# A planner that counts a port shared by VectorE and GpSimd, with other durations and priorities; the splitting of token blocks on VectorE; a reordered end of a token block

## The chip, the core and the metric

The kernel runs on one core of one Trainium2 chip. The metric is the device time of one execution in microseconds (us), from the first to the last thing that the core does; smaller is better. The engines of the core are TensorE (PE in the rows; PEld is its weight load), VectorE (DVE), ScalarE (ACT), GpSimd (POOL) and SyncE (SP). SP computes nothing here: it issues almost all DMAs. Each engine works through its own list of instructions in order; between engines there are only semaphores.

## What is computed

Windowed attention (8 batches, 8 heads, 576 positions, 64 channels a head; four heads with a plain causal window of 32, four with a dilated one), then a mixing by two Fourier transforms, a normalisation, and a feed-forward layer (512 to 2048 to 512) with the residual added:

```python
scores = scale * np.matmul(q, k.transpose(0, 1, 3, 2))
scores = np.where(masks[None, :, :, :], scores, -1000000000.0)
scores = scores - np.max(scores, axis=-1, keepdims=True)
attn = np.exp(scores)
attn = attn / (np.sum(attn, axis=-1, keepdims=True) + 1e-09)
x = matmul(attn, v)                       # then (batch, seq, 512)
...
X = np.fft.fft(np.fft.fft(x, axis=1), axis=2)
u = x + np.real(X).astype(np.float32)
mu = np.mean(u, axis=-1, keepdims=True)
var = np.mean((u - mu) ** 2, axis=-1, keepdims=True)
un = (u - mu) / np.sqrt(var + 1e-06)
ch = np.maximum(un @ w_ch1, 0.0) @ w_ch2
return (u + ch).astype(np.float32)
```

## The kernel before

**Stages.** `attention` (L481) does each batch in twelve units (`attend`, L504): two score products into a bank `sc`, a masked minimum on VectorE (L521), exponentials on ScalarE (L527), four transposes (L540), a copy, four products with `v` (L547) and a division on VectorE, stored to DRAM. `mix` (L648) reads a batch back, folds it on GpSimd and VectorE, multiplies it by sequence and channel tables (`seq_sb`, `tail_sb`, `chn_sb`, `alt_sb`), and adds the result on GpSimd; `normalise` (L605) writes the rows `u`, with mean and scale in two more columns, to DRAM. The products are kept accurate by splitting each float32 operand in a rounded high part (a copy on ScalarE) and the remainder (a subtraction on VectorE or GpSimd); three products make one.

**The feed-forward layer** is in two parts. Five of the 16 hidden blocks (`wa1`, `wa2`) are done in the `fill` pieces (L1087), two token tiles each, as soon as their tiles are normalised; the sums go to DRAM as `parts`. The other eleven are done at the end for nine token blocks of 512 rows, in a loop over pairs of hidden blocks (`two_tiles`, L1227; `one_tile`, L1259) that uses sums and differences of halves of the tokens and of the weights to save products. The weights arrive as 64-bit words, and `words_of` (L834) makes float32 of them with four VectorE instructions (L857 to L866).

**A token block.** `load_blocks` (L1056) reads the 512 rows of a block in four DMAs (L1014), transposes them with four VectorE instructions (L1024), makes four sums or differences (`combine`, L1068, GpSimd), and splits seven pieces into `xb`: ScalarE makes each high part (L1078), and the remainder (L1081) is made by GpSimd for three pieces and by VectorE for four. `xb` exists once, so a piece is overwritten when its last product of the block before is done. For the first token block this has a late priority (`LAST`), for the others an early one (`SOON`).

**The end of a token tile** (`finish`, L963): the rows `u` come by DMA (L977, or an indirect one from GpSimd, L980), ScalarE adds the mean back (L983), the partial sums come by DMA (L985). When PE has closed the accumulation `acc`, VectorE adds acc and the partial sums (L986), and then multiplies by the row's scale and adds u (L988). The output DMAs follow: for the last block 16 of 64 KB, half on SP's queue, half on ScalarE's.

**The order of all work** is made on the host by a planner (`Plan`, L178): each `add` gives an engine, an estimated cost, what is read and written, a priority (smaller goes first) and, for a DMA, its bytes. `run` (L235) plays the program through in time: an engine that is free takes the ready operation of smallest priority number. A DMA is taken to land after 0.65 us, its bytes at 300 GB/s behind the DMAs before it, and 2.8 us. The lists of instructions of each engine are written in the order in which the planner started them; on the chip nothing else of the planned times is kept. The priority of attention is 12 b + u for unit u of batch b. That of other work is set against it by constants (L37 to L41): `P_QK0`, `P_QK`, `P_V` for loads of q, k, v; `P_W + P_WF f` for preparing the five fill weights f, whose DMAs have `P_WD` added; `P_MIX*` and `P_SPAN*` for the place and the length of a mix; `P_FILL` for the first fill. `T_SEQ` and `T_CHN` are the planned times from which the tables may be loaded (L470 to L477); these loads are in GpSimd's queue, which has nothing before them, and no semaphore holds them.

Of the kernel before, what the change touches and what calls it, by code (L numbers as in the profile page):

```python
# [19 lines left out]
P = 128  # L20
# [153 lines left out]
class Op:  # L174
    __slots__ = ("eng", "cost", "fn", "prio", "bufs", "after", "waits", "ready", "start", "num", "nbytes")


class Plan:  # L178
# [20 lines left out]
    def add(self, eng, cost, fn, r=(), w=(), prio=0.0, nbytes=0, at=0.0):  # L199
        op = Op()  # L200
        op.eng, op.cost, op.fn, op.prio, op.nbytes = eng, cost, fn, prio, nbytes
# [33 lines left out]
    def run(self):  # L235
# [15 lines left out]
        lanes = {e: [] for e in busy}  # L251

# [20 lines left out]
        while events:  # L273
# [67 lines left out]
def pe(n, m=P):  # L341
    return max(n / 2400 + 0.0025, m / 1200)
# [25 lines left out]
def fused_kernel(ctx: ExitStack, tc, q, k, v, w1, w2, seq, tail, chn, alt, mask, ident, perm, flip, out):  # L368
# [67 lines left out]
    def dma(fn, r, w, prio, nbytes, slow=1):  # L436
        return add("SP", 0.5, fn, r, w, prio, nbytes * slow)
# [3 lines left out]
    def start():  # L441
        dma(lambda: nc.sync.dma_start(out=mask_sb(), in_=mask), (), (mask_sb,), -7.9, QB * 3 * KB * 4)
        dma(lambda: nc.sync.dma_start(out=ident_sb(), in_=ident), (), (ident_sb,), -7.8, P * 3 * P * 4)
        dma(lambda: nc.sync.dma_start(out=perm_sb(), in_=perm), (), (perm_sb,), -7, QB * QB * 12)
# [33 lines left out]


# [24 lines left out]
    def attend(b, dil, j, u, tq, kb, vt, xt, prio):  # L504
# [3 lines left out]
        for n, t in enumerate(blocks):  # L508
# [7 lines left out]
            add("PE", 2 * pe(512), scores, (tq, kb), ((sc, n),), prio)  # L516
# [29 lines left out]
        for i in range(4):  # L546
            add("PE", 0.16, lambda i=i: nc.tensor.matmul(  # L547
# [57 lines left out]
    def normalise(u, idx, prio):  # L605
# [15 lines left out]
            out=uc()[:, C + 1:C + 2], in0=r0(), in1=r1(), op=ALU.mult), (r0, r1), ((uc, 2),), prio + 1)  # L621
# [693 lines left out]
```

## Time and profile before

| what | us |
|---|---|
| three runs: median (lowest to highest) | 1122.07 (1121.26 to 1122.24) |
| the profiled execution, whole | 1123.04 |
| the profiled execution, span of its instructions | 1121.3 |
| PE busy in that span | 1072.7 |
| VectorE, ScalarE, GpSimd busy | 726.6, 522.5, 289.4 |
| mean granted PE clock | 0.981 of full |

The profiled execution took 1.74 us more than its span and 0.97 us more than the median run. A row of the chip's trace names a line of the kernel, an engine, the operation, what it writes and reads, how many instructions were merged, and in brackets how long the engine was idle before it and what released it. The granted clock has two levels, 2.4 GHz (1.00 in the rows) and 1.2 GHz (0.50); a mean between them says how long each was granted in the stretch.

### The profile page before, as it was taken

Reading aid. Unit: us, or ns where it says so; the run is one execution under the profiler, and the core shown is the slowest. Engines: PE = TensorE matmul, PEld = TensorE weight load, DVE = VectorE, ACT = ScalarE, POOL = GpSimd, SP = SyncE. Lnnn points to the kernel's source line nnn. Section 1 sums busy time; section 2 is a strip of 40 time slices with the busy share of each in tenths; the row PEclk is TensorE's granted clock in tenths of the full one; section 3 lists DMA queues with packets and bytes.
Section 4 is the critical chain, followed back from the end, with each engine's and each line's share of the span. In section 5 each row is a group of like instructions: output and inputs, shape, how many; then the busy total and the mean of one; then the engine's idle time right before and its main releaser. Section 6 shows DMA issues by size and latency. Waiting matters only on the chain.

```text
span 1121.3 us, 20217 instructions
## 1 busy us (share of the span) xinstructions
PE 1072.7 (96%) x7066; PEld 948.1 (85%) x7066; DVE 726.6 (65%) x2318; ACT 522.5 (47%) x1331; POOL 289.4 (26%) x341
## 2 busy tenths in 40 slices
PE   5799999999999999999989899999999999999997
PEld 3567888889888988899978798898988889888886
DVE  5789988767867778867769763536363545454523
ACT  4587656546555634344435443333333333333331
POOL 2025365343434254300030421121202120212200
PEclk8799999999999999999999899999999999999999
DMA  9677567656655344345423250505050504041211
GB/s 313 175 207 220 159 193 195 193 143 184 176 165 149 115 136 123 110 122 152 129 87 114 66 160 1 150 1 151 1 150 1 142 9 132 20 107 45 93 59 38
DMA packets 104310, 137.05 MB, mean 122 GB/s; under 512 B 9656, under 2 KB 62328, under 8 KB 104208
## 3 DMA queue, kind: packets, MB, share of 16 engines
q1 hardware_dynamic: 100624, 126.85, 39.0%
q0 software_dynamic: 3040, 8.09, 2.4%
q8 instruction: 56, 0.92, 0.3%
q10 hardware_dynamic: 544, 0.82, 0.2%
q14 instruction: 46, 0.38, 0.1%
HBM read 97.92 MB, written 37.80 MB: 121 GB/s over the span
## 4 chain that ended last, share of the span: by engine, by line
PE 81%; DVE 11%; DMA 3%; issue 2%; POOL 1%; ACT 1%; SPq 0%; DVEq 0%; ACTq 0%; POOLq 0%
PE sc L942 15%; PE ff L1199 13%; PE mix L1199 8%; PE ff L926 7%; PE pt L942 6%; PE av L942 6%; PE ff L942 6%; PE sc L513 5%; PE av L547 5%; PE mix L775 2%; PE pt L540 2%; PE mix L729 2%; PE pt L926 2%; DVE pm L521 2%; DMA ut<-in_w_dram 1%
## 5 line engine op out<-in xcount | busy, mean ns | idle before, releaser
L527 ACT ACTIVATE pm<-pm,mx 96x128 f32<-96x128 f32 x384 | 130.3, 394 | 53.6 <-DVE mx L521 49.9
L1215 ACT COPY s<-ff 128x256 f32<-128x256 f32 x135 | 50.2, 373 | 163.9 <-PE ff L1199 163.5
L513 PE MATMUL sc<-kb,tq 128*96 128x256 f32 x384 | 109.4, 405 | 16.2 <-DMA kb<-in_k_dram 8.0
L926 PE MATMUL ff<-ut,wa 128*128 128x256 f32 x780 | 110.0, 291 | 3.3 <-DVE h L934 3.3
L521 DVE CUSTOM_DVE_ANT_0 pm<-sc,mask_sb 96x128 f32<-96x128 f32 x384 | 92.8, 278 | 24.4 <-PE sc L513 23.4
L942 PE MATMUL sc<-wa,h 128*128 128x512 f32 x420 | 106.4, 395 | 0.0
L926 PEld LDWEIGHTS ff<-ut,wa 128*128 128x128 f32 x780 | 99.7, 192 | 5.1 <-DVE h L934 3.9
L942 PE MATMUL ff<-wa,h 128*128 128x512 f32 x390 | 95.8, 397 | 0.0
L547 PEld LDWEIGHTS av<-vt,ptsb 128*96 128x96 f32 x768 | 79.9, 171 | 16.7 <-issue 5.5
L1068 POOL TENSOR_TENSOR ut<-ut 128x512 f32<-128x512 f32 x36 | 50.7, 1428 | 166.5 <-DVE ut L1024 86.4
L547 PE MATMUL av<-vt,ptsb 128*96 128x65 f32 x768 | 84.5, 253 | 6.9 <-DVE xt L559 5.3
L942 PEld LDWEIGHTS sc<-wa,h 128*128 128x128 f32 x420 | 76.2, 188 | 15.6
L942 PEld LDWEIGHTS ff<-wa,h 128*128 128x128 f32 x390 | 71.6, 188 | 15.7
L942 PE MATMUL sc<-wd,h 128*128 128x512 f32 x324 | 84.1, 394 | 0.0
L513 PEld LDWEIGHTS sc<-kb,tq 128*96 128x96 f32 x384 | 57.9, 173 | 30.0 <-issue 13.3
L1246 DVE TENSOR_TENSOR c<-s,s 128x256 f32<-128x256 f32 x45 | 22.3, 496 | 89.6 <-ACT s L1215 86.5
L1199 PEld LDWEIGHTS ff<-xb,pair 128*128 128x128 f32 x540 | 74.0, 189 | 6.6 <-ACT s L1215 0.7
L1024 DVE STREAM_TRANSPOSE ut<-ut 128x512 f32<-128x512 f32 (+1 forms) x76 | 71.7, 984 | 11.0 <-DMA ut<-us 10.9
L1199 PE MATMUL ff<-xb,pair 128*128 128x256 f32 x540 | 76.8, 281 | 0.5 <-ACT s L1215 0.5
L1081 POOL TENSOR_TENSOR xb<-ut,xb 128x512 fp32r<-128x512 f32 x27 | 36.8, 1363 | 133.5 <-ACT xb L1078 133.5
L1220 ACT ACTIVATE h<-row 128x256 fp32r<-128x256 f32 x90 | 37.5, 417 | 64.1 <-DVE row L1236 38.2
L980 POOL DMA_INDIRECT ut<-us,flip_sb x20 | 19.8, 988 | 180.9 <-DMA ut<-us 87.2
(158 smaller groups left out, 2318.4 us busy)
## 6 DMA issues: line engine op xcount, KB each, us to landing
vt<-in_v_dram SPq DMA_DIRECT2D x32, 390.0 KB
ut<-in_w_dram SPq DMA_DIRECT2D x20, 512.0 KB
us<-uc SPq DMA_DIRECT2D x36, 257.0 KB
tq<-in_q_dram SPq DMA_DIRECT2D x32, 288.0 KB
part<-row SPq DMA_DIRECT2D x36, 256.0 KB
ut<-us SPq DMA_DIRECT2D x36, 256.0 KB
ut<-part SPq DMA_DIRECT2D x36, 256.0 KB
kb<-in_k_dram SPq DMA_DIRECT2D x62, 144.0 KB
```

The source lines that it names most:

```text
L513: nc.tensor.matmul(sc()[:QB, 256 * n:256 * n + 256], lhsT=tq()[:, cols], rhs=kb()[:, :, keys], start=True, stop=True,)
L521: nc.vector.tensor_tensor_reduce(pm()[:, i], sc()[:QB, KB * i:KB * i + KB], mask_sb()[:, masks[blocks[i // 2]]], -0.125, 3.0e38, ALU.add, ...
L527: add("ACT", 0.295, lambda i=i: nc.scalar.activation(out=pm()[:, i], in_=pm()[:, i], func=AF.Exp, bias=mx()[:, i:i + 1], scale=-1.0), ((mx ...
L547: add("PE", 0.16, lambda i=i: nc.tensor.matmul(av()[:QB, 65 * i:65 * i + 65], lhsT=pt()[:, i], rhs=vt()[:, i % 2, blocks[i // 2]], start=T ...
L926: nc.tensor.matmul(z()[:, :n_tok], lhsT=wf()[:, a, kk], rhs=ut()[:, p, kk], start=(kk == 0 and n == 0), stop=(kk == KT - 1 and n == 2),)
L942: nc.tensor.matmul(acc(), lhsT=h()[:, a, P * s:P * s + P], rhs=wf()[:, p], start=(first and n == 0), stop=(last and n == 2),)
L1024: nc.vector.transpose(out=o[back], in_=x[:, g])
L1068: add("POOL", pool(C), lambda: nc.gpsimd.tensor_tensor(out=made(i)(), in0=x(), in1=y(), op=ALU.subtract), (*done, *((raw, ("s", j)) for j ...
L1081: add(eng, (pool if eng == "POOL" else dve)(C), lambda j=j, get=get, lo=lo: lo.tensor_tensor(out=xb()[:, j, 1], in0=get(), in1=xb()[:, j, ...
L1199: nc.tensor.matmul(z()[:, lo:lo + TOK1], lhsT=ap()[:, a, kk], rhs=xb()[:, j, p, kk], start=(start and k == 0), stop=(stop and k == 6 * len ...
L1215: add("ACT", act(TOK1), lambda: nc.scalar.copy(out=s(), in_=src()[:, :TOK1]), (src,), (s,), SOON - 1)
L1220: add("ACT", act(TOK1), lambda: nc.scalar.activation(out=h()[:, 0], in_=z(), func=AF.Relu), need, ((h, 0),), SOON)
```

## The change

No product and no token is added or left out. The change has five parts.

1. **Port.** An operation can carry the mark `port`: all computing of GpSimd has it, and many VectorE operations whose operands are all in SBUF. In the planner an operation with the mark starts only when no other marked one is running. No semaphore is added for it on the chip.
2. **Durations.** Several costs are other numbers; a DMA is taken to land after 0.45 us, its bytes at 340 GB/s and 0.6 us; a transpose of a token tile costs 1.0 in place of 0.6, and its loads count 1.25 times.
3. **Constants.** Nearly all priorities are other numbers. The mask and the identity now stand before, or level with, the first q. The mix of batch 0 is spread over 18.58 units in place of 8, later ones over 18.65 in place of 13. Fill weights start at 10.04, 9.28 apart, in place of 8.0 and 8.0.
4. **Tables.** Ahead of each table load VectorE writes one element of the table (`touch`), planned from `T_SEQ` (10.36) or `T_CHN` (24.62) on; GpSimd's DMA waits for it by semaphore.
5. **Token blocks.** All four `combine` and all seven remainders of `load_blocks` are VectorE's. In `finish` VectorE first makes partial sums times scale plus u, which needs no `acc`, and then acc times scale plus that.

The diff, cut to its core ("..." marks what is left out; marks and costs of the same kind as those shown are left out elsewhere):

```diff
-P_QK0, P_V0 = -8.0, -7.0
-P_ST, P_FD, P_WD, P_ST0, P_FD0, P_SPAN0, P_SPAN1 = -4.0, -12.0, -10.0, 0.0, 0.0, 8.0, 13.0
-P_QK, P_V, P_TR, P_MIX, P_SPAN, P_W, P_WF, P_FILL, P_FILLT = -8.0, -7.0, -5.0, 2.0, 13.0, 8.0, 8.0, 45.0, 4.0
-P_MIX0, P_MIX1 = 3.0, 0.0
-T_SEQ, T_CHN = 16.0, 24.0
+P_QK0, P_V0 = -7.8, -7.0
+P_ST, P_FD, P_WD, P_ST0, P_FD0, P_SPAN0, P_SPAN1 = -4.0, -21.87, -10.68, 0.0, 0.0, 18.58, 12.39
+P_QK, P_V, P_TR, P_MIX, P_SPAN, P_W, P_WF, P_FILL, P_FILLT = -8.0, -5.77, -5.0, 2.0, 18.65, 10.04, 9.28, 43.42, 4.0
+P_MIX0, P_MIX1 = 3.0, 0.93
+T_SEQ, T_CHN, T_STEP, P_SEQ, P_CHN = 10.36, 24.62, 1.0, -4.0, -2.0
+P_MASK, P_ID, P_PERM = -7.9, -7.8, -7.0
...
+        op.port = port or (eng == "POOL" and not nbytes)
...
-                        if place(ops[e[1]], now):
+                        if (not ops[e[1]].port or port <= now) and place(ops[e[1]], now):
...
+                    if got.port:
+                        port = end
...
-                        dma = max(dma, end + 0.65) + got.nbytes / 3.0e5
-                        done = dma + 2.8
+                        dma = max(dma, end + 0.45) + got.nbytes / 3.4e5
+                        done = dma + 0.6
...
+        def table(t, m, dst, src, prio, nbytes, at):
+            def touch():
+                nc.vector.memset(dst().bitcast(F32)[0:1, 0:1] if m is None else dst().bitcast(F32)[0:1, 0, 0:1], 0.0)
+            key = t if m is None else (t, m)
+            add("DVE", 0.065, touch, (), (key,), prio, at=at)
+            add("POOL", 0.53, lambda: nc.gpsimd.dma_start(out=dst(), in_=src), (), (key,), prio, nbytes)
+
         for i in range(2):
             for m in range(2):
-                add("POOL", 0.06, lambda i=i, m=m: nc.gpsimd.dma_start(out=seq_sb[i]()[:, m], in_=seq[i, m]),
-                    (), ((seq_sb[i], m),), 6 + i, P * 2 * NSP * 4, at=T_SEQ + i)
+                table(seq_sb[i], m, lambda i=i, m=m: seq_sb[i]()[:, m], seq[i, m], P_SEQ + i, P * 2 * NSP * 4, T_SEQ + i * T_STEP)
...
-        add("DVE", dve(C), lambda: nc.vector.tensor_tensor(
-            out=row(), in0=acc(), in1=row(), op=ALU.add), (acc,), (pk,), prio)
         add("DVE", 0.66, lambda: nc.vector.scalar_tensor_tensor(
-            row(), row(), u(C + 1, C + 2), u(0, C), op0=ALU.mult, op1=ALU.add), (uk,), (pk,), prio)
+            u(0, C), row(), u(C + 1, C + 2), u(0, C), op0=ALU.mult, op1=ALU.add), (pk,), (uk,), prio, port=True)
+        add("DVE", 0.66, lambda: nc.vector.scalar_tensor_tensor(
+            row(), acc(), u(C + 1, C + 2), u(0, C), op0=ALU.mult, op1=ALU.add), (uk, acc), (pk,), prio)
...
-                tuple((us[c], i0 + i) for i in range(n)), ((rb, ("raw", a)),), prio, 32 * 4 * n * 512)
+                tuple((us[c], i0 + i) for i in range(n)), ((rb, ("raw", a)),), prio, 32 * 4 * n * 512, slow=1.25)
...
-                add("DVE", 0.6 / len(steps), lambda i=i, g=g, back=back: turn(i, g, back), raws, done[-1:], prio)
+                add("DVE", 1.0 / len(steps), lambda i=i, g=g, back=back: turn(i, g, back), raws, done[-1:], prio)
...
-            add("POOL", pool(C), lambda: nc.gpsimd.tensor_tensor(out=made(i)(), in0=x(), in1=y(), op=ALU.subtract),
-                (*done, *((raw, ("s", j)) for j in after)), ((raw, ("s", i)),), prio)
+            add("DVE", dve(C), lambda: nc.vector.tensor_tensor(out=made(i)(), in0=x(), in1=y(), op=ALU.subtract),
+                (*done, *((raw, ("s", j)) for j in after)), ((raw, ("s", i)),), prio, port=True)
...
-            lo = nc.gpsimd if eng == "POOL" else nc.vector
-            add(eng, (pool if eng == "POOL" else dve)(C), lambda j=j, get=get, lo=lo: lo.tensor_tensor(
+            add("DVE", dve(C), lambda j=j, get=get: nc.vector.tensor_tensor(
                 out=xb()[:, j, 1], in0=get(), in1=xb()[:, j, 0].bitcast(F32), op=ALU.subtract),
-                (*need, (xb, (j, 0))), ((xb, (j, 1)),), prio)
+                (*need, (xb, (j, 0))), ((xb, (j, 1)),), prio, port=True)
...
-    def put_h(z, need):
+    def put_h(z, need, port=True):
```

## Rows read from the trace of the kernel before

**Rows 1.** The page's first part: busy time of an engine, its share of the span, and its instructions.

```profile
PE 1072.7 (96%) x7066; PEld 948.1 (85%) x7066; DVE 726.6 (65%) x2318; ACT 522.5 (47%) x1331; POOL 289.4 (26%) x341
```

**Rows 2.** Busy time by stretch, the whole span in eleven stretches: the stretch and its length in us; busy us and instructions of PE, PEld, DVE, ACT, POOL; then the mean granted PE clock, the busy share of the DMA engines, and GB/s.

```profile
0.00:8.04 8.04, 0.00 (x1) 0.03 (x1) 4.91 (x23) 1.28 (x1) 4.67 (x12) 1.00 0.85 225
8.04:36.00 27.96, 20.11 (x101) 14.74 (x102) 17.06 (x81) 14.10 (x37) 1.08 (x2) 0.80 1.07 309
36.00:84.00 48.00, 42.21 (x264) 31.75 (x263) 35.62 (x215) 34.97 (x103) 6.11 (x9) 0.87 0.63 188
84.00:240.00 156.00, 149.51 (x1147) 131.16 (x1146) 133.39 (x622) 99.46 (x277) 78.31 (x106) 1.00 0.64 187
240.00:430.00 190.00, 189.42 (x1375) 169.09 (x1374) 139.77 (x619) 102.47 (x282) 74.94 (x110) 1.00 0.54 156
430.00:560.00 130.00, 125.89 (x794) 112.63 (x794) 102.66 (x209) 54.11 (x122) 17.34 (x22) 0.99 0.40 120
560.00:590.00 30.00, 24.40 (x154) 22.21 (x154) 20.64 (x30) 13.08 (x32) 11.52 (x7) 0.94 0.26 88
590.00:630.00 40.00, 40.00 (x251) 35.86 (x250) 37.99 (x84) 20.80 (x53) 0.00 (x0) 1.00 0.42 119
630.00:645.00 15.00, 12.01 (x52) 10.08 (x51) 9.85 (x13) 6.04 (x12) 11.63 (x8) 0.77 0.08 19
645.00:1110.00 465.00, 465.00 (x2925) 417.58 (x2924) 219.48 (x420) 176.17 (x420) 83.76 (x69) 1.00 0.26 74
1110.00:1121.30 11.30, 4.10 (x18) 2.98 (x16) 5.22 (x8) 0.00 (x0) 0.00 (x0) 0.81 0.33 93
```

**Rows 3.** Instructions in order of time, from the start to 24 us: start, length, engine, line, operation, what it writes and reads, count, idle time before it and what ended that.

```profile
1.25 1.29 POOL L472 DMA_DIRECT2D seq<-in_seq_dram  x2 [0.82 <-POOLq L1303]
...
5.15 1.34 SPq L498 DMA_DIRECT2D tq<-in_q_dram  x1
...
8.04 2.84 PE L513 MATMUL sc<-kb,tq 128*96 128x256 f32 x6 [8.04 <-DMA kb<-in_k_dram]
...
9.64 3.23 SPq L854 DMA_DIRECT2D ut<-in_w_dram  x2
...
16.23 0.64 PE L513 MATMUL sc<-kb,tq 128*96 128x256 f32 x2 [1.89 <-DMA tq<-in_q_dram]
...
22.98 0.43 DVE L857 TENSOR_SCALAR ut<-ut 128x512 uint32<-128x512 uint32 x1 [3.87 <-DMA ut<-in_w_dram]
...
23.88 0.67 PE L513 MATMUL sc<-kb,tq 128*96 128x256 f32 x2 [2.91 <-DVE mx L521]
```

**Rows 4.** The issues of DMAs by line: what is written and read, the issuing queue, count, KB of each, and the median us from issue to landing.

```profile
seq<-in_seq_dram POOLq DMA_DIRECT2D x4, 290.0 KB, 9.5
```

**Rows 5.** Instructions in order of time, 559 to 571 us, of VectorE, GpSimd and PE; columns as in rows 3.

```profile
559.81 4.11 DVE L1081 TENSOR_TENSOR xb<-ut,xb 128x512 fp32r<-128x512 f32 x3
559.95 5.12 POOL L1068 TENSOR_TENSOR ut<-ut 128x512 f32<-128x512 f32 x3 [79.54 <-ACT xb L1078]
...
563.85 1.52 DVE L857 TENSOR_SCALAR ut<-ut 128x512 uint32<-128x512 uint32 x1
...
566.97 1.75 DVE L860 SCALAR_TENSOR_TENSOR ut<-ut 128x512 uint32<-128x512 uint32 x1
...
568.75 1.64 DVE L863 SCALAR_TENSOR_TENSOR ut<-ut 128x512 uint32<-128x512 uint32 x1
...
570.77 2.91 PE L926 MATMUL pt<-ut,wa 128*128 128x256 f32 x12 [5.14 <-DVE h L934]
```

**Rows 6.** The same for 630 to 640 us.

```profile
630.76 4.39 POOL L1068 TENSOR_TENSOR ut<-ut 128x512 f32<-128x512 f32 x3 [59.24 <-DVE ut L1024]
...
632.52 1.51 DVE L1222 SCALAR_TENSOR_TENSOR h<-row,h 128x256 fp32r<-128x256 f32 x1
...
636.68 2.93 PE L1199 MATMUL ff<-xb,tailw 128*128 128x256 f32 x12 [2.99 <-ACT h L1220]
```

**Rows 7.** Single lines over the whole run: count, and ns of one instruction as least, median and most; then first and last start.

```profile
L1081 DVE TENSOR_TENSOR xb<-ut,xb x36: 681/690/1799, 559.8 to 1050.5; 128x512 fp32r<-128x512 f32 x36
L863 DVE SCALAR_TENSOR_TENSOR ut<-ut x20: 677/684/1639, 27.3 to 631.1; 128x512 uint32<-128x512 uint32 x20
L857 DVE TENSOR_SCALAR ut<-ut x20: 410/418/1519, 23.0 to 621.3; 128x512 uint32<-128x512 uint32 x20
L1222 DVE SCALAR_TENSOR_TENSOR h<-row,h x90: 378/425/1509, 589.1 to 1102.6; 128x256 fp32r<-128x256 f32 x90
```

**Rows 8.** Instructions in order of time around 280 us, SyncE's queue and VectorE: the four loads of one group of token rows, and the transposes that read them.

```profile
279.96 1.81 SPq L1014 DMA_DIRECT2D ut<-us  x4
...
285.35 2.09 DVE L1024 STREAM_TRANSPOSE ut<-ut 128x512 f32<-128x512 f32 x2 [3.03 <-DMA ut<-us]
```

**Rows 9.** Instructions in order of time at the end of the span.

```profile
1112.04 1.40 DVE L986 TENSOR_TENSOR ut<-sc,ut 128x512 f32<-128x512 f32 x2 [4.05 <-PE sc L942]
...
1112.55 0.86 PE L942 MATMUL pt<-wa,h 128*128 128x512 f32 x3
1113.24 0.85 PE L942 MATMUL av<-wa,h 128*128 128x512 f32 x3
...
1114.12 4.23 SPq L999 DMA_DIRECT2D out_dram<-ut  x8
...
1115.88 1.40 DVE L988 SCALAR_TENSOR_TENSOR ut<-ut 128x512 f32<-128x512 f32 x2
```

More of the change, by code (lines that the diff above doesn't have):

```diff
@@ L174 @@
 class Op:
-    __slots__ = ("eng", "cost", "fn", "prio", "bufs", "after", "waits", "ready", "start", "num", "nbytes")
+    __slots__ = ("eng", "cost", "fn", "prio", "bufs", "after", "waits", "ready", "start", "num", "nbytes", "port")
 class Plan:
@@ L197, in buf, with add @@
         return b
-    def add(self, eng, cost, fn, r=(), w=(), prio=0.0, nbytes=0, at=0.0):
+    def add(self, eng, cost, fn, r=(), w=(), prio=0.0, nbytes=0, at=0.0, port=False):
         op = Op()
+        op.port = port or (eng == "POOL" and not nbytes)
         op.eng, op.cost, op.fn, op.prio, op.nbytes = eng, cost, fn, prio, nbytes
@@ L251, in run @@
         lanes = {e: [] for e in busy}
+        port = 0.0
         def place(o, now):
@@ L341, in pe, with pe4 @@
 def pe(n, m=P):
-    return max(n / 2400 + 0.0025, m / 1200)
+    return max(n / 2327 + 0.0067, m / 1200)
+def pe4(n):
+    return n / 600 + 0.0035
 def act(n):
@@ L546, in attend @@
         for i in range(4):
-            add("PE", 0.16, lambda i=i: nc.tensor.matmul(
+            add("PE", 0.17, lambda i=i: nc.tensor.matmul(
                 av()[:QB, 65 * i:65 * i + 65], lhsT=pt()[:, i],
@@ L620, in normalise @@
         add("DVE", 0.07, lambda: nc.vector.tensor_tensor(
-            out=uc()[:, C + 1:C + 2], in0=r0(), in1=r1(), op=ALU.mult), (r0, r1), ((uc, 2),), prio + 1)
+            out=uc()[:, C + 1:C + 2], in0=r0(), in1=r1(), op=ALU.mult), (r0, r1), ((uc, 2),), prio + 1, port=True)
         dma(lambda: nc.sync.dma_start(out=u_rows(idx), in_=uc()), (uc,), ((us[idx // 4], idx % 4),), prio + 1, P * 2056)
@@ L627, in turned @@
         for kk in range(KT):
-            add("PE", 0.109, lambda kk=kk: nc.tensor.transpose(
+            add("PE", 0.12, lambda kk=kk: nc.tensor.transpose(
                 tp()[:, P * kk:P * kk + P], uc()[:, kk:C:KT],
@@ L874, in halves @@
             out=ap()[:, 1], in0=shape(get()), in1=ap()[:, 0].bitcast(F32), op=ALU.subtract),
-            (*need, (of, ("b", i, 0))), ((of, ("b", i, 1)),), prio)
+            (*need, (of, ("b", i, 0))), ((of, ("b", i, 1)),), prio, port=True)
     def prep(rows, three, dst, t, gate, prio):
@@ L902, in combine @@
             add("DVE", dve(256), lambda: nc.vector.tensor_tensor(out=made(i)(), in0=x(), in1=y(), op=op),
-                need + tuple((t0, ("s", j)) for j in after), ((t0, ("s", i)),), prio)
+                need + tuple((t0, ("s", j)) for j in after), ((t0, ("s", i)),), prio, port=True)
         if n == 1:
@@ L1051, in tokens @@
                 out=part(1), in0=tv()[:, src], in1=part(0).bitcast(F32), op=ALU.subtract),
-                (*done, (ut, (0, k0))), ((ut, (1, k0)),), prio)
+                (*done, (ut, (0, k0))), ((ut, (1, k0)),), prio, port=True)
     xb = Buf()
@@ L1073, in load_blocks @@
         combine(3, plain(1, 0), made(1), (1,))
-        both = ((3, made(0), 0, "POOL"), (4, made(1), 1, "POOL"), (6, made(3), 3, "POOL"), (0, plain(0, 0), None, "DVE"),
-                (1, plain(1, 0), None, "DVE"), (5, made(2), 2, "DVE"), (2, plain(1, 1), None, "DVE"))
-        for j, get, s, eng in both:
+        both = ((3, made(0), 0), (4, made(1), 1), (6, made(3), 3), (0, plain(0, 0), None),
+                (1, plain(1, 0), None), (5, made(2), 2), (2, plain(1, 1), None))
+        for j, get, s in both:
             need = done if s is None else [(raw, ("s", s))]
@@ L1223, in put_h @@
             h()[:, 1], z(), 0.0, h()[:, 0].bitcast(F32), op0=ALU.max, op1=ALU.subtract),
-            (*need, (h, 0)), ((h, 1),), SOON)
+            (*need, (h, 0)), ((h, 1),), SOON, port=port)
         return h
@@ L1246, in two_tiles @@
         add("DVE", dve(TOK1), lambda: nc.vector.tensor_tensor(
-            out=c22(), in0=s3(), in1=s5(), op=ALU.add), (s3, s5), (c22,), SOON)
+            out=c22(), in0=s3(), in1=s5(), op=ALU.add), (s3, s5), (c22,), SOON, port=True)
         h22 = put_h(lambda: c22(), (c22,))
```

45 lines of the change are left out of this document (22 added, 23 removed).

## The prediction

> **What bounds the kernel now.** First the page's busy times: PE works 1072.7 of 1121.3 us and the next engine, VectorE, 726.6 [rows 1]. The change leaves PE's products as they are, so it can win only what PE loses. PE loses in two ways: it idles, or it works while the lower clock is granted. The view that shows both is the busy time by stretch [rows 2]. Idle time is a stretch's length less PE's busy time; what the lower clock costs I estimate as busy time times one minus the mean granted clock.
>
> - 0 to 8 us: 8.0 idle.
> - 8 to 36: 7.9 idle, 20.1 x 0.20 = 4.0 by the clock: 11.9.
> - 36 to 84: 5.8 idle, 42.2 x 0.13 = 5.5: 11.3.
> - 84 to 560: 6.5 + 0.6 + 4.1 idle, 125.9 x 0.01 = 1.3: 12.5.
> - 560 to 645: 5.6 + 3.0 idle, 24.4 x 0.06 + 12.0 x 0.23 = 4.3: 12.9.
> - 645 to 1110, 465 us with eight of nine token blocks: none.
> - the end: 7.2 idle.
>
> Together 64 us; the reader should see that 20 of them lie before 36 us, 31 before 84, and none in the long last stage. Then I read, in order of time, why PE waits in the start, in 559 to 571, in 630 to 640 and at the end [rows 3, 5, 6, 9].
>
> **The change, part by part.** The sum is made against the profiled execution (1123.04 us); the median is 0.97 below it.
>
> *Start, 0 to 8 us: -2.5.* PE waits for the first k until 8.04 [rows 3]. By then 225 GB/s x 8.04 = 1.81 MB have moved [rows 2], which at the 309 GB/s of the next stretch is 5.9 us; so some 2.2 us pass before transfers run. Among these bytes are tables: GpSimd issues them from 1.25 us on [rows 3], 290 KB each for the sequence tables [rows 4]. The change holds all tables until about 10 us. Then the first product's k and q (0.59 MB by the shapes in the code), with mask and identity ahead of q, are 0.93 MB, or 1.44 MB if the permutations and the first v share the engines: 3.0 to 4.7 us, so PE starts between 5.2 and 6.9. I take 5.5, nearer the first, because k has a queue of its own. Bounds: -3, and +0.5 if q's later place in the queue counts fully.
>
> *8 to 36 us: -4.* The same tables make the next two waits. A q issued at 5.15 releases PE only at 16.23; weight words issued at 9.64 release VectorE at 22.98, and VectorE, waiting in order, holds up PE for 2.91 us [rows 3]. All tables are 2.82 MB by their shapes, 9.1 us at 309 GB/s, and a sequence table takes 9.5 us to land [rows 4]. The change moves them behind the first attention loads, and moves the first weight words from priority -2.0 to -0.64. But the bytes stay inside this stretch, whose DMA engines are full (1.07), and PE, once it has waited, is granted the lower clock. So I take a third of the 11.9. Bounds: -9, all but one wait gone; +4, the tables now delaying later q and k as they did the first.
>
> *36 to 84 us: -3.* Neither DMA (0.63) nor VectorE (35.6 of 48) is full here [rows 2]; PE waits because of the order on VectorE. A fill weight costs VectorE two times about 0.42 + 4 x 0.69 = 3.2 us (the medians of L857 and L1081, whose shape the others have [rows 7]). The constants put the five 9.28 apart and the first mix over 18.58 units, so attention is interrupted less. No row shows the new order; bounds -9 and +5, a quarter taken.
>
> *84 to 560 us: -1.* VectorE has 133.4 of 156 us up to 240, and 102.7 of 130 from 430 on [rows 2]. The change removes nothing here; the marks only order VectorE and GpSimd better in the plan, and no semaphore keeps that order on the chip. Bounds -8 and +8.
>
> *560 to 645 us: -9.* GpSimd's subtractions of a token block and VectorE's own take turns here. While GpSimd works, three remainders take 4.11 us, L860 1.75 and L863 1.64 [rows 5], against 0.69 each at L1081's median; at 632 an h remainder takes 1.51 [rows 6], against 0.42 [rows 7]. PE waits 5.14 us for h behind them, and 2.99 us the second time. In the rows of 559 to 571 the excess is 4.11 - 2.07 + 1.10 + 1.06 + 0.95 = 5.2 us; the seven instructions that VectorE takes over cost 7 x 0.69 = 4.8 us in a block. So VectorE's total stays, but each h waits for one instruction of 0.69 and not for one of 1.5 to 1.8, and h has the earlier priority. I take 9 of the 12.9; bounds -12.9 and 0.
>
> *An operation of one SBUF operand.* L857, with one SBUF input and no second tensor, took 1.52 [rows 5], so it is disturbed too. The Trainium skill (SBUF — State Buffer, "Who interferes with whom") says that the port pair is held for a whole instruction, that a VectorE instruction with at most one SBUF input contends only in its two-port modes, and that `tensor_scalar` has these. By that rule, which the row bears out, the marks on `tensor_scalar` are right, and the sum stays.
>
> *645 to 1110 us: 0.* VectorE works 219 of 465 us [rows 2]. Seven more instructions in each of seven further blocks are 7 x 7 x 0.69 = 34 us, which brings it from 47 to 54%; PE, never idle here, covers it with the eight `down` products queued between a block's last product and the next. If the cover were gone at each block's end, at about 1 us each: +8.
>
> *End: -2.* The last product ends at 1114.09; VectorE still has two additions and the multiplications, to 1117.28 [rows 9]. After the change only one instruction follows each tile's product; with the tiles 0.70 apart on PE and 0.70 on VectorE it ends near 1114.9. SP's eight issues took 4.23 us from 1114.12. Beginning near 1112.8 they would end at 1117.0 at that pace, 1.3 earlier; when they follow VectorE, near 1115.9, 2.4 earlier. The first extra instruction of a tile (0.7) runs before its product ends. The total VectorE work of `finish` stays. Bounds -2.4 and -1.3.
>
> *At nothing.* Six `touch` writes are well under 1 us of VectorE in the first 30 us; behind the held table loads GpSimd's queue has nothing before the first mix, which needs the tables anyway. In `finish` the first instruction now waits for u as well; queued behind it on VectorE are the next block's h, and for these waits ScalarE and then PE. In the long last stage that has the cover above.
>
> Sum: -2.5 - 4 - 3 - 1 - 9 + 0 - 2 = -21.5, so 1101.5 for the profiled execution and 1100.5 for the median.
>
> **The rivals.**
>
> *The stalls of the first half only move.* The tables and weights still fill the DMA engines until about 36 us, the plan's better durations are lost in what it can't see, and 8 to 560 us gain nothing. For it: 1.07 DMA share to 36 us, and no semaphore for the port. Against: the two longest waits come behind table bytes. -2.5 - 9 - 2 = -13.5: 1108.5.
>
> *VectorE becomes the bound at 560 to 645.* It has 38.0 of 40 us in 590 to 630 with GpSimd idle [rows 2]; the second block's 4.8 us and the weights then push each other, and PE waits for weights where it waited for h. -12.5: 1109.5. With the rival before it: -4.5, 1117.5.
>
> *Planned landings that are too early (slower).* The plan now lets a DMA land 1.05 us and its bytes after its issue, against 3.45 before. Four loads of a group of token rows then look done 4 x 0.46 + 0.45 + 0.48 + 0.6 = 3.4 us after the first issue. The trace has 5.4 [rows 8], and that with VectorE already waiting 3.0. VectorE will be told to transpose 2.0 us too early, in 16 groups before 560 us: 32 us of waiting, with everything behind it. PE pays if no fill products cover it. Against: from 240 to 430, where such a wait stands [rows 8], PE idles 0.6 us in all [rows 2]. If PE pays for all 32 and the first half gains nothing else: -13.5 + 32 = +18.5, 1140.5; it turns the result from where PE pays 13.5 of the 32, some 0.85 us a group.
>
> The Trainium skill (DMA: Bandwidth & Descriptors, "Anatomy of one DMA") gives a DMA from GpSimd's queue about 2.0 us beside its bytes. By that figure, which speaks against the plan's 1.05, a group is estimated at 1.8 + 0.3 + 2.0 = 4.1 us, 0.7 later than planned, and the 32 us become about 12; the row at 280 us, with 5.4, is above both.
>
> *More than I take.* The start gains near its bounds: -3 - 9 - 7 - 4 - 11 - 2.4 = -36: 1086.
>
> **How the numbers follow.** Chances: the forecast, 1100.5 (own range 1092 to 1106), 0.45; first half only moved, 0.15; VectorE the bound late, 0.13; both, 0.08; landings too early, 0.11; more, 0.08. The forecast stands because the three terms that rest on rows of a named cause (start, 560 to 645, end) make 13.5 of the 21.5. The range leaves out the slower rival and a part of the largest gain: 1086 to 1118. About 0.2% (2.2 us) is what a measurement of this kernel can tell from no change. Faster by more: 0.45 + 0.15 + 0.13 + 0.06 + 0.08, less a little for a weak slower mechanism beside them: 0.84; within: 0.05; slower: 0.11.
>
> **What would show it.** Start: PE's first product before 6 us, and no table issue before it. 8 to 36: no PE wait over 1 us on q, and VectorE not waiting 3 us for weight words. 560 to 645: L1068 and L1081 on VectorE at about 0.69, L860 and h there never above 0.9, PE idle below 3 us. End: under 1 us from the last product to VectorE's last instruction. The forecast is wrong if VectorE's waits on L1024's loads grow beyond their present few us and PE's idle time between 84 and 560 us grows with them, or if a block's end after 645 us shows PE idle.

## The result: slower by 0.6%, and where the time went

The changed kernel takes 1129.29 us (median of 4 runs, 1127.05 to 1132.00) against 1122.15 for the kernel before, measured beside it (1121.26 to 1123.67): ratio 1.0061, 95% interval 1.0041 to 1.0081. The forecast was 1100.5 us, with a range of 1086 to 1118. The profiled run took 1127.05 us, its span 1125.3. Line numbers after 480 are 11 to 13 higher than before (L1024 is L1037, L1068 is L1081, L1081 is L1093, L1199 is L1211, L1222 is L1234, L1253 is L1265); in e1, e6 and e7 they are one higher still.

Busy time by stretch of the changed kernel, columns as in [rows 2]:

```profile
0.00:8.04 8.04, 1.72 (x4) 1.24 (x5) 4.91 (x23) 1.28 (x1) 0.19 (x4) 1.00 0.80 226
8.04:36.00 27.96, 22.48 (x134) 16.17 (x132) 19.36 (x122) 18.97 (x53) 5.89 (x10) 0.88 1.00 295
36.00:84.00 48.00, 44.85 (x342) 35.57 (x343) 43.90 (x242) 42.28 (x120) 9.40 (x13) 1.00 0.93 278
84.00:240.00 156.00, 146.43 (x1060) 127.31 (x1057) 120.64 (x553) 86.86 (x243) 66.83 (x92) 0.98 0.58 167
240.00:430.00 190.00, 183.26 (x1316) 158.61 (x1315) 140.09 (x618) 101.81 (x281) 80.21 (x112) 1.00 0.50 142
430.00:560.00 130.00, 126.61 (x814) 113.76 (x814) 98.37 (x217) 51.59 (x117) 22.61 (x30) 1.00 0.46 130
560.00:590.00 30.00, 29.68 (x190) 26.62 (x189) 25.90 (x55) 17.69 (x42) 0.00 (x0) 1.00 0.41 143
590.00:630.00 40.00, 39.31 (x246) 34.95 (x245) 37.67 (x81) 19.68 (x49) 0.00 (x0) 1.00 0.34 89
630.00:645.00 15.00, 14.20 (x86) 12.26 (x85) 10.21 (x19) 7.58 (x16) 2.03 (x2) 1.00 0.37 124
645.00:1110.00 465.00, 454.58 (x2843) 406.48 (x2842) 230.55 (x462) 169.27 (x410) 17.13 (x18) 1.00 0.25 71
1110.00:1125.30 15.30, 10.16 (x52) 8.17 (x50) 3.69 (x6) 0.77 (x2) 0.00 (x0) 0.96 0.24 70
```

Read as before (idle, and busy time by what the clock lacks), 8 to 84 us and 560 to 645 us lose much less than before. 84 to 560 us lose more, and so do 645 to 1110 us, which had lost nothing. The idle time misses products that start late while their row still counts as busy. So the table has a second measure: each kind of product is priced at its undisturbed spacing (the lower third of the distances from start to start in both traces), and a stretch's loss is its time less the price of the products started in it. By it the difference of the spans (+4.0) comes out whole. Both measures come from one profiled run of each kernel.

| stretch, us | forecast (bounds) | idle and clock: before, after | loss by spacing: before, after | difference |
|---|---|---|---|---|
| 0 to 8 | -2.5 (-3, +0.5) | 8.0, 6.3 | 7.8, 7.2 | -0.6 |
| 8 to 36 | -4 (-9, +4) | 11.9, 8.2 | 15.9, 11.6 | -4.3 |
| 36 to 84 | -3 (-9, +5) | 11.3, 3.2 | 15.8, 7.5 | -8.3 |
| 84 to 560 | -1 (-8, +8) | 12.5, 22.6 | 28.0, 44.7 | **+16.7** |
| 560 to 645 | -9 (-12.9, 0) | 12.9, 1.8 | 13.9, 3.1 | -10.8 |
| 645 to the last product | 0 (0, +8) | 0, 10.4 | 1.5, 14.8 | **+13.3** |
| end | -2 (-2.4, -1.3) | 7.2, 5.1 | 7.2, 5.1 | -2.1 |

**What came as forecast.** At the start, in order of time (answers to [rows 3]):

```profile
6.32 2.85 PE L526 MATMUL sc<-kb,tq 128*96 128x256 f32 x6 [6.32 <-DMA tq<-in_q_dram]
...
13.11 1.29 POOL L485 DMA_DIRECT2D seq<-in_seq_dram  x2 [12.67 <-DVE mx L534]
```

PE starts 1.7 us earlier, now released by q, and the first table is issued after it. Two single lines over the whole run (answers to [rows 7]), and PE's waits in 560 to 645 us (total, times, longest):

```profile
L1093 DVE TENSOR_TENSOR xb<-ut,xb x63: 682/691/708, 568.7 to 1054.6; 128x512 fp32r<-128x512 f32 x63
...
L1234 DVE SCALAR_TENSOR_TENSOR h<-row,h x90: 406/423/441, 583.8 to 1108.6; 128x256 fp32r<-128x256 f32 x90
```

```profile
PE ff L1211 <- DVE h L1234: 0.8, 1, 0.8
PE ff L1211 <- ACT s L1227: 0.7, 1, 0.7
PE pt L939 <- DVE h L947: 0.3, 1, 0.3
```

No remainder takes more than 0.71 us, no h more than 0.44 (1.80 and 1.51 before), and the waits of 5.14 and 2.99 us in [rows 5, 6] are gone. The end, answers to [rows 9]:

```profile
1118.89 3.62 SPq L1012 DMA_DIRECT2D out_dram<-ut  x8
...
1119.31 0.85 PE L955 MATMUL av<-wa,h 128*128 128x512 f32 x3
...
1120.20 0.75 DVE L1001 SCALAR_TENSOR_TENSOR ut<-av,ut 128x512 f32<-128x512 f32 x1
```

VectorE is done 0.8 us after the last product ends (3.2 before).

**What did not.** PE's waits in 645 to 1110 us; the kernel before has none there:

```profile
PE mix L1211 <- DVE row L1265: 8.8, 7, 2.2
PE ff L1211 <- ACT s L1227: 1.6, 1, 1.6
```

Seven times, once in a block, PE waits for the same sum `row`. One of them, in order of time (SyncE's queue, VectorE, PE), first in the changed kernel, then the same place in the kernel before:

```profile
703.21 2.26 SPq L1016 DMA_DIRECT2D out_dram<-ut  x5
...
705.57 2.03 SPq L1027 DMA_DIRECT2D ut<-us  x4
...
712.82 2.09 DVE L1037 STREAM_TRANSPOSE ut<-ut 128x512 f32<-128x512 f32 x2 [3.74 <-DMA out_dram<-ut]
...
714.83 0.38 DVE L1258 TENSOR_TENSOR c<-s,s 128x256 f32<-128x256 f32 x1
715.13 2.07 DVE L1037 STREAM_TRANSPOSE ut<-ut 128x512 f32<-128x512 f32 x2
...
717.75 0.42 DVE L1265 TENSOR_TENSOR row<-s,mix 128x256 f32<-128x256 f32 x1
...
718.22 0.97 PE L1211 MATMUL mix<-xb,pair 128*128 128x256 f32 x6 [0.78 <-DVE row L1265]
```

```profile
711.50 2.03 SPq L1014 DMA_DIRECT2D ut<-us  x4
...
720.47 0.41 DVE L1253 TENSOR_TENSOR row<-s,mix 128x256 f32<-128x256 f32 x1
...
720.79 1.09 DVE L1024 STREAM_TRANSPOSE ut<-ut 128x512 f32<-128x512 f32 x1
```

The four loads of the next block's rows are issued at 705.57. The plan has them landed 0.46 + 0.45 + 4 x 0.96 + 0.6 = 5.4 us later (256 KB each, counted 1.25 times, at 340 GB/s, with no transfer before them); VectorE gets them after 7.25, having stood idle for 3.74. All four transposes and then `row` are queued behind that wait, and PE, which needs `row` for its next product, stops. In the kernel before `row` comes ahead of the transposes, and these come 9.3 us after the issue, without a wait. The row at 712.82 names an output write as what released VectorE. By the landing times in the same trace that is not so: the latest output write, issued at 707.70, landed at 713.21, when VectorE was at work again, and the fourth load at 712.64. At each of the seven borders the fourth load lands 0.2 us before the transposes start. A block takes 59.9 us on average from its first product to the next block's (637.8 to 1057.0 for seven), against 58.3 before (645.0 to 1052.9). At the first such border the changed kernel was 7.2 us ahead, at its last product it is 6.1 behind. Over the whole run VectorE's idle time before the transposes is (releaser, us, times):

```profile
  DMA ut<-us: 22.9, 14
  DMA out_dram<-ut: 22.0, 5
  DMA part<-row: 4.2, 1
```

That is 49 us, 29.8 of them at these seven borders; the kernel before had 10.9 in six waits, all of them before 560 us. Where these rows name another DMA than `ut<-us`, the fourth load had landed 0.1 to 0.2 us before the transposes all the same.

### The profile page after: what moved, and what is told of

Its sections match the earlier page's. It is cut to its first block, busy times and chain, and to the rows that moved or that the text cites. A ratio compares the mean times of both kernels' runs of the same rounds, so it can differ in the third digit from the quotient of the medians.

```text
span 1125.3 us, 20175 instructions
## 1 busy us (share of the span) xinstructions
PE 1073.3 (95%) x7066; PEld 941.2 (84%) x7066; DVE 735.3 (65%) x2391; ACT 517.8 (46%) x1331; POOL 204.3 (18%) x278
## 5 line engine op out<-in xcount | busy, mean ns | idle before, releaser
L526 PE MATMUL sc<-kb,tq 128*96 128x256 f32 x384 | 107.9, 394 | 10.6 <-DMA tq<-in_q_dram 9.0
L534 DVE CUSTOM_DVE_ANT_0 pm<-sc,mask_sb 96x128 f32<-96x128 f32 x384 | 93.2, 279 | 29.4 <-PE sc L526 25.8
L1037 DVE STREAM_TRANSPOSE ut<-ut 128x512 f32<-128x512 f32 (+1 forms) x76 | 72.0, 987 | 49.2 <-DMA ut<-us 22.9
L560 PEld LDWEIGHTS av<-vt,ptsb 128*96 128x96 f32 x768 | 77.4, 166 | 17.2 <-issue 4.7
L1211 PEld LDWEIGHTS ff<-xb,pair 128*128 128x128 f32 x540 | 73.9, 189 | 8.1 <-ACT s L1227 2.0
L1211 PE MATMUL ff<-xb,pair 128*128 128x256 f32 x540 | 77.0, 281 | 1.6 <-ACT s L1227 1.6
L1211 PE MATMUL mix<-xb,pair 128*128 128x256 f32 x486 | 68.1, 282 | 8.8 <-DVE row L1265 8.8
L1211 PEld LDWEIGHTS mix<-xb,pair 128*128 128x128 f32 x486 | 61.6, 190 | 10.4 <-DVE row L1265 10.4
L955 PEld LDWEIGHTS sc<-wd,h 128*128 128x128 f32 x324 | 57.1, 188 | 9.8
```

Of the source, the lines that this page charges most:

```text
L526: nc.tensor.matmul(sc()[:QB, 256 * n:256 * n + 256], lhsT=tq()[:, cols], rhs=kb()[:, :, keys], start=True, stop=True,)
L534: nc.vector.tensor_tensor_reduce(pm()[:, i], sc()[:QB, KB * i:KB * i + KB], mask_sb()[:, masks[blocks[i // 2]]], -0.125, 3.0e38, ALU.add, ...
L560: add("PE", 0.17, lambda i=i: nc.tensor.matmul(av()[:QB, 65 * i:65 * i + 65], lhsT=pt()[:, i], rhs=vt()[:, i % 2, blocks[i // 2]], start=T ...
L955: nc.tensor.matmul(acc(), lhsT=h()[:, a, P * s:P * s + P], rhs=wf()[:, p], start=(first and n == 0), stop=(last and n == 2),)
L1037: nc.vector.transpose(out=o[back], in_=x[:, g])
L1211: nc.tensor.matmul(z()[:, lo:lo + TOK1], lhsT=ap()[:, a, kk], rhs=xb()[:, j, p, kk], start=(start and k == 0), stop=(stop and k == 6 * len ...
```

## The experiments

Theory L: the new landing time of a DMA in the plan, 0.6 us after its bytes where it was 2.8, is too early, and engines that work in order stand before loads that have not come. Rivals: P (the port marks force a worse order), V (seven more VectorE instructions in a block are too many), C (the new constants harm 84 to 430 us). Runs of before beside these had medians of 1122.0 to 1122.3. "To 645" is the loss by spacing up to 645 us of the profiled run, "block" the mean distance of one block start from the next, over the last eight starts. These two columns come from one profiled run of each kernel, which lies off the kernel's median by up to 4.6 us (e1 4.6 above, e6 4.3 above, the changed kernel 2.2 below), so that a few us between two values of "to 645" show nothing.

| kernel | median us (runs) | ratio to before, 95% | to 645 | block |
|---|---|---|---|---|
| before | 1122.15 (4) | | 81.5 | 58.3 |
| changed | 1129.29 (4) | 1.0061, 1.0041 to 1.0081 | 74.2 | 59.9 |
| e1 block landings later | 1120.23 (10) | 0.9978, 0.9955 to 1.0001 | 83.6 | 58.3 |
| e2 all landings 2.8 | 1092.79 (4) | 0.9726, 0.9710 to 0.9742 | 53.2 | 58.3 |
| e3 no marks | 1147.06 (4) | 1.0207, 1.0174 to 1.0239 | 91.0 | 60.2 |
| e4 before, blocks on VectorE | 1110.01 (4) | 0.9887, 0.9871 to 0.9904 | 67.6 | 58.3 |
| e5 before, landing 0.6 | 1165.24 (4) | 1.0372, 1.0341 to 1.0402 | 112.6 | 59.8 |
| e6 only token rows 2.8 | 1112.97 (4) | 0.9919, 0.9901 to 0.9937 | 75.2 | 58.4 |
| e7 only the others 2.8 | 1124.87 (8) | 1.0025, 1.0004 to 1.0046 | 71.5 | 60.7 |
| e8 2.8, old constants | 1093.34 (4) | 0.9745, 0.9728 to 0.9762 | 55.0 | 58.3 |
| e9 all landings 4.0 | 1090.44 (4) | 0.9719, 0.9702 to 0.9735 | 53.2 | 58.3 |
| e12 all landings 1.7 | 1097.38 (4) | 0.9794, 0.9774 to 0.9815 | 54.9 | 58.4 |
| e10 2.8, no marks | 1099.19 (4) | 0.9790, 0.9767 to 0.9813 | 59.8 | 58.3 |
| e11 2.8, tables not held | 1100.43 (4) | 0.9815, 0.9799 to 0.9832 | 59.8 | 58.3 |

**e1: the four loads of a later token block land 4 us later in the plan.**

```diff
-                        done = dma + 0.6
+                        done = dma + 0.6 + got.late
...
-        done = turned_tokens(c, 0, 4, (raw, lambda: words(raw)), (tr, lambda: words(tr)), prio)
+        done = turned_tokens(c, 0, 4, (raw, lambda: words(raw)), (tr, lambda: words(tr)), prio, 4.0 if c else 0.0)
```

> The changed kernel, but in the plan alone the four loads of a token block (blocks 2 to 9) land 4.0 us later; no other estimate and no instruction is other. Theory L (landings planned too early: VectorE reaches the transposes before their rows have come, and what is queued behind them is late for PE): VectorE's waits before the block transposes go from about 4 us to under 1 us a block, the pitch of a token block from 59.9 us to 58.3 as before the change, and the time falls by 9 to 13 us, to about 1118. Theory V (the seven instructions that VectorE took over are the cost of the last stage): the pitch stays near 59.9 and the time near 1129.

The wait of the last stage goes: VectorE waits before no transpose there, and of PE's waits from 645 to 1110 us one is left,

```profile
PE ff L1212 <- ACT s L1228: 1.2, 1, 1.2
```

and blocks stand 58.3 us apart. The median is 9 us below the changed kernel's, not the 13.3 of the table: the profiled run gives up 9.4 us more before 645 us, where no estimate was edited but the planner's order came out another. Much of that may be the runs, the profiled one being 4.6 us above e1's median and that of the changed kernel 2.2 below its own. The ten runs spread over 11.5 us, so the size is uncertain; the place is not.

**e2: every DMA lands 2.8 us after its bytes, as before.**

```diff
-                        done = dma + 0.6
+                        done = dma + 2.8
```

> The changed kernel, but every DMA in the plan lands 2.8 us after its bytes, as before the change, in place of 0.6; all else as changed. Theory L: both losses go, the one of the last stage and the one of 84 to 560 us, where PE waits at the first sequence products of a mix; 15 to 25 us less than the changed kernel, 1104 to 1114. Theory P (the port marks spread a mix out in the plan and cost 84 to 560 us): only the last stage is won back, 1116 to 1120. Theory V: nothing, near 1129.

More than L expected: 36.5 us below the changed kernel with one number put back. PE stands in no row of waits from 645 us on: its busy time there (columns as in [rows 2]) is

```profile
645.00:1079.00 434.00, 434.00 (x2728) 389.80 (x2728) 217.95 (x439) 162.98 (x391) 16.11 (x17) 1.00 0.24 69
```

**e3: no port marks.**

```diff
-        op.port = port or (eng == "POOL" and not nbytes)
+        op.port = False
```

> The changed kernel with no operation marked for the port; all else as changed. Theory L: within 4 us of the changed kernel either way, since waits for DMAs stay. Theory P: 84 to 560 us win 10 to 17 us back, 1112 to 1119.

18 us slower, so P falls. L, which had expected less than 4 us either way, missed as well: the marks do work (see e10). One line over the run, first of the changed kernel and then of e3 (ns as least, median, most):

```profile
L707 DVE TENSOR_TENSOR oo<-t,t x24: 411/416/420, 61.9 to 455.2; 128x256 f32<-128x256 f32 x16, 32x256 f32<-32x256 f32 x8
```

```profile
L707 DVE TENSOR_TENSOR oo<-t,t x24: 409/417/965, 64.9 to 453.5; 128x256 f32<-128x256 f32 x16, 32x256 f32<-32x256 f32 x8
```

Without marks three of these 24 instructions fall together with one of GpSimd's in the trace and take 0.95 to 0.97 us.

**e4: the kernel before with part 5's token blocks on VectorE alone.**

```diff
-            add("POOL", pool(C), lambda: nc.gpsimd.tensor_tensor(out=made(i)(), in0=x(), in1=y(), op=ALU.subtract),
+            add("DVE", dve(C), lambda: nc.vector.tensor_tensor(out=made(i)(), in0=x(), in1=y(), op=ALU.subtract),
...
-        both = ((3, made(0), 0, "POOL"), (4, made(1), 1, "POOL"), (6, made(3), 3, "POOL"), (0, plain(0, 0), None, "DVE"),
+        both = ((3, made(0), 0, "DVE"), (4, made(1), 1, "DVE"), (6, made(3), 3, "DVE"), (0, plain(0, 0), None, "DVE"),
```

> The kernel before with one part of the change alone: all eleven sums, differences and remainders of a token block on VectorE, at the planner's old costs. Theory L: the old landings keep VectorE from waiting, PE stays without idle time after 645 us, and 560 to 645 us lose 8 to 11 us less than before: 1111 to 1114. Theory V: the last stage loses 1.5 us a block, so 1122 to 1127.

12.1 us faster than before, a little more than expected, and the blocks stay 58.3 us apart: V falls, and the step "560 to 645 us: -9, then 0" holds when it is alone.

**e5: the kernel before with the new landing alone** (0.45, 340 GB/s, 0.6).

> The kernel before with the new landing alone (0.45 us, bytes at 340 GB/s, 0.6 us); marks, costs, constants, tables and token blocks as before. Theory L (the landings planned too early are what loses the time): slower than before by 15 to 35 us, 1137 to 1157, with more waiting of VectorE for the loads of token rows and of the first sequence products of a mix for their folds. Rival C (the new constants lose the time between 84 and 430 us): within 5 us of before, 1117 to 1127.

43 us slower, more than L's 35: C falls, the old constants suffer from it no less. PE's waits in the last stage are those of the changed kernel again (old line numbers):

```profile
PE mix L1199 <- DVE row L1253: 8.0, 7, 2.0
```

**e6 and e7: later landing for the loads of token rows only, and for all SyncE DMAs but these.** `late` is 2.2 in `turned_tokens` in e6, and in every other `dma` in e7.

```diff
-                        done = dma + 0.6
+                        done = dma + 0.6 + got.late
```

> The changed kernel with the landing of the loads of token rows alone, in the fill pieces and in the token blocks, 2.2 us later in the plan (0.6 + 2.2). Theory L-rows (these loads carry the loss): most of the 36 us by which the later landing of all DMAs was faster, 1093 to 1105. Theory L-others (reads of a mix, partial sums, rows u and weights carry it): the last stage's 13 us at most, 1116 to 1126. Rival C: 1116 to 1126 as well, and the next kernel brings nothing either.

> The changed kernel with 2.2 us more landing for every DMA of SyncE's queue except the loads of token rows. Theory L-rows: 1120 to 1132, blocks still near 59.9 us apart. Theory L-others: 1100 to 1112, the loss between 84 and 430 us back to some 20 us, blocks still 59.9 apart. Rival C: 1124 to 1134.

Neither theory in its pure form: 16.3 and 4.4 us gained, 20.7 together, where both at once (e2) gain 36.5. The last stage is repaired by e6 alone (58.4 against 60.7). In 84 to 560 us, by the spacing, e6 loses 1 us less than the changed kernel, e7 10 less and e2 22 less; e7 gives up 7 elsewhere before 645 us. So the token rows alone do not carry the loss of that stretch. VectorE's waits in 84 to 430 us, first e6, then e7:

```profile
DVE ee L706 <- POOL t L694: 17.7, 10, 5.5
...
DVE ut L1038 <- DMA ut<-us: 7.7, 4, 3.5
```

```profile
DVE ut L1038 <- DMA ut<-us: 14.4, 7, 3.4
...
DVE ee L706 <- POOL t L694: 2.5, 3, 1.1
```

The changed kernel has 6.7 us before the folds of a mix (`ee`) and 15.0 before the token rows (`ut`), e2 3.8 and 6.6. In e6 the wait for the rows is halved, and VectorE stands before the folds instead (GpSimd, which makes them, waited 34.4 us for their reads, in e2 29.6). In e7 the wait for the folds shrinks, and that for the rows stays. That e6's wait moves because the later transposes bring the folds forward in the plan is a guess from these rows and not shown.

**e8: e2 with the old constants** for mixes, fill weights and v.

> The changed kernel with the landing of all DMAs at 2.8 us, and with the old constants for the mixes, the fill weights and v (spans 8 and 13, weights from 8.0 on and 8.0 apart, first fill at 45); tables, marks, costs and token blocks as changed. With the new constants this took 1092.8. Theory L alone (constants are worth little): 1090 to 1098. Theory K (the constants bring most of what 8 to 84 us gained, some 10 us): 1100 to 1106. Rival C (the new constants harm): below 1090.

0.5 us from e2: these constants are worth nothing that can be measured here.

**e9 and e12: landings of 4.0 and 1.7 us.**

> The changed kernel with every DMA landing 4.0 us (in place of 0.6) after its bytes in the plan; with 2.8 it took 1092.8. Theory L, as a threshold (once planned landings are not earlier than real ones, more brings nothing): 1088 to 1096. Rival T (any later landing helps further, because it spreads the loads out): below 1086. Rival S (too late is as bad as too early: engines take other work first and the loads' readers come late): above 1098.

> The same with 1.7 us, midway between 0.6 (1129.3) and 2.8 (1092.8). Theory L: groups of token rows that take 5.4 us to land are still planned some 1 us too early, so 1102 to 1118, and blocks after 645 us between 58.3 and 59.9 apart. If the loss were a matter of a lucky order and not of the landing, any time from 1090 to 1130 would do, without order between the three values.

With 0.6, 1.7, 2.8 and 4.0 the time is 1129.3, 1097.4, 1092.8, 1090.4: it falls steeply and levels off, as L's threshold has it, and e9 and e2, whose intervals overlap, are the fastest kernels of the study, some 30 us ahead of the kernel before. But 1.7 gains more than L's own sum allowed. VectorE waits there nearly as long as with 0.6 (one wait of e12, to be held against 705 to 718 us above):

```profile
742.76 2.06 SPq L1027 DMA_DIRECT2D ut<-us  x4
...
750.37 1.11 DVE L1037 STREAM_TRANSPOSE ut<-ut 128x512 f32<-128x512 f32 x1 [3.89 <-DMA ut<-us]
...
753.36 0.41 DVE L1265 TENSOR_TENSOR row<-s,mix 128x256 f32<-128x256 f32 x1
753.69 2.08 DVE L1037 STREAM_TRANSPOSE ut<-ut 128x512 f32<-128x512 f32 x2
```

The idle time is 3.89, more than the 3.74 of the changed kernel. Yet `row` now stands ahead of the last two transposes, 3.0 us behind the start of the first and not 4.9, and PE does not wait. At these two borders it is not the length of VectorE's wait that counts, but how far behind it the instruction stands that PE needs.

The trace also gives the time at which each load had landed, and so how early the plans were. In the changed kernel the fourth load of a group for a `fill` piece landed 4.0 to 8.6 us after the first issue (16 groups, median 4.7), of a token block 7.0 to 8.3. Worked out as above, the plan has 3.4 and 5.4 with 0.6 us, 4.5 and 6.5 with 1.7, 5.6 and 7.6 with 2.8, 6.8 and 8.8 with 4.0; the kernel before had planned 5.7 and 7.4. Of the 25 groups in that trace all landed later than the plan with 0.6 has them, some 18 later than with 1.7, 4 later than with 2.8 and 1 later than with 4.0: the time levels off with that count.

**e10: e2 without marks.**

> The changed kernel with 2.8 us landing and without any port mark. With the marks it took 1092.8; with landings of 0.6 us the marks were worth 18 us. Theory P+ (the marks are worth something by themselves, since a planned duration that the port stretches makes every later planned time early): 1100 to 1112. Theory L alone (the marks only made up for early landings): 1091 to 1096.

6.4 us slower than e2, between what L and P+ had expected: the marks are worth something by themselves, a third of the 18 that they are worth when landings are planned too early. By what path stays open: the time by which instructions exceed 1.15 times the median of their kind adds up to 11.9 us on VectorE (e2 11.6) and 10.6 on GpSimd (e2 6.0).

**e11: e2 without the six writes,** so that no semaphore holds the tables.

```diff
-            add("DVE", 0.065, touch, (), (key,), prio, at=at)
-            add("POOL", 0.53, lambda: nc.gpsimd.dma_start(out=dst(), in_=src), (), (key,), prio, nbytes)
+            add("POOL", 0.53, lambda: nc.gpsimd.dma_start(out=dst(), in_=src), (), (key,), prio, nbytes, at=at)
```

> The changed kernel with 2.8 us landing and without the six writes that hold the table loads, so that GpSimd issues the tables from about 1.3 us on, as before. With them it took 1092.8. If holding the tables is worth what was forecast for 0 to 36 us: 1097 to 1101, with the first product at 8 us. If only PE's first start moves and the bytes are paid for anyway: 1092 to 1095.

```profile
1.25 1.30 POOL L484 DMA_DIRECT2D seq<-in_seq_dram  x2 [0.82 <-POOLq L1314]
...
8.78 2.84 PE L525 MATMUL sc<-kb,tq 128*96 128x256 f32 x6 [8.78 <-DMA tq<-in_q_dram]
```

7.6 us slower: holding the tables is worth about what was forecast for 0 to 36 us, though by the losses by spacing only 3.5 of it lie there (e11 8.0 + 16.9, e2 7.4 + 14.0) and 5.5 in 36 to 84 us.

## Why the prediction was wrong

**Without the landing the sum had the right sign and was 8 us too small; the landing, kept as a rival of 0.11, decides.** Against before, e2 gains 29.4 us. The parts measured singly are the token blocks 12.1 (e4), the tables 7.6 (e11), the marks 6.4 (e10), the end 2.1 (the traces) and the constants 0.5 (e8): 28.7. They were measured in different surroundings, so that their sum is a check and no proof, and the other durations of part 2 were not tried singly. The forecast had 21.5 for all, in other shares: by the spacing e2 gains 2 us in 8 to 36 us (forecast 4), 7 in 36 to 84 (3), 5 in 84 to 560 (1) and 13 in 560 to 645 (9). The landing then takes 36.5 us back, and what is left is slower by 7.

**The step that failed first: "84 to 560 us: -1".** Its price weighed the marks alone and said that the change removes nothing here; that the plan's landing has changed stood only in a rival. Measured +16.7, outside its bounds; with the landing alone put back (e2) the stretch loses some 22 us less, 5 less than before the change. The reason given against the rival, that PE idled little where such a wait stands [rows 8], took one wait's cover for that of sixteen groups: the plan of before had them late enough (5.7 us for a group) that VectorE waited at only six of its 25 groups.

**The step that failed second: "645 to 1110 us: 0".** It counted 34 us of VectorE's work against PE's queue, and this part held (e4). It did not ask what the landing does to the loads of the token blocks, which are four DMAs as well; the rival too was priced for 16 groups "before 560 us". Measured +13.3 against a bound of +8, and not at a block's end, as feared, but some 20 us into it, where the next block's rows come. The mechanism stands in [rows 8] already: loads that land after 5.4 us, planned for 3.4.

**The rival "planned landings that are too early"** names the cause. Its size was about half right (it had PE pay for up to 32 us before 560), and its point of decision (0.85 us a group) was passed: 16.7 us over 16 groups is 1.04 if all of the loss is put down to them. But it priced the token rows alone, and these alone do not carry it: e6, which moves them, gives back 1 us of that stretch, e7, which moves the reads of a mix and the rest, 10. What it also lacked was the last stage, and its chance was too small: the plan's number had changed for every DMA of the program, and one row already spoke against it.

The Trainium skill (DMA: Bandwidth & Descriptors, "Anatomy of one DMA") gives a fixed cost of about 2.0 us for a DMA of GpSimd's queue. The plan's 0.45 + 0.6 lies below it, 0.45 + 1.7 just above. For SyncE's queue, of which the page does not speak there, the trace agrees: the first 128 KB load of [rows 8] landed 2.4 us after its issue, its bytes included. Between the two plans the time falls by 32 us.

**Terms that were right but mis-sized.** 0 to 8 us: -0.6 for -2.5; q, behind mask and identity, releases PE at 6.32, outside the 5.5 taken but within 5.2 to 6.9. 8 to 36: -4.3 for -4, in part by luck: one of its signs failed, PE waiting 2.7 us for a second q (its waits for q by 36 us are 9.0 in two, the longer 6.3), and e2, with the same tables, gains 2. 36 to 84: -8.3 for -3, and more from the tables than from the constants that were named: e2 loses 8.4 us there, with tables not held 13.9 (e11), with the old constants 11.5 (e8). 560 to 645: -10.8 for -9, by the mechanism named. End: -2.1 for -2.

**The marks.** "No semaphore keeps that order on the chip" was taken as a reason for little. The order holds well enough to count: L707 above is never stretched with them (though L876, 0.68 us at the median, still takes up to 1.10), and e10 gives 6.4 us.

## What to carry to other kernels

In a kernel whose order is planned ahead, a duration that is planned too short can be far dearer than one too long: here 0.6 us of landing cost 36.5 us, and 4.0 cost nothing against 2.8. When a change touches a number that every transfer uses, price it for every group of transfers in every stage, the long quiet one too. And look at what stands in the queue behind a wait: much the same wait of VectorE (3.74 and 3.89 us) cost PE a stop in one order and nothing in another.

## What the runs showed of the hardware that was not expected

Four loads of 256 KB issued within 2.03 us were in VectorE's hands 7.25 us after the first issue (705.57 to 712.82), having landed 3.2, 4.7, 6.0 and 7.1 us after it. The DMA engines were 0.71 busy between 705 and 720 us (0.25 over the whole stage), and five output writes had been issued on the same queue from 703.21 on. With 128 KB a load it was 5.4 us [rows 8].

Two kernels with the same instructions and another order differ in how steady they are: ten runs of e1 spread over 11.5 us, four of e2 over 3.0; thirteen of before spread over 4.6. Why is not shown.
